# An attention and two-MLP kernel with an early expert pass: seven buffers for words to convert, evenly spaced conversions, earlier transposes, 240 rows

## The chip, the core and the metric

The kernel runs on one core of a Trainium2 chip. The core has five engines, each with its own queue that is worked off in order: PE (matrix multiply), DVE (vector), ACT (activations), POOL (GpSimd) and SP, which here only issues DMA transfers. The metric is the device time of one execution in microseconds (us), taken as the median of several runs.

## What is computed

The inputs are drawn once; two of the weights, `moe2_w_in` and `moe2_w_out`, come as float64. Cut to what matters:

```
scores = q @ k^T / 8; scores below (row maximum - tau) are masked; softmax; attn @ v      # 4 x 8 heads, 576 x 64
x = attention output as 2304 tokens x 512
logits = x @ w_gate; e = argmax(logits) over 8 experts; gate = softmax(logits)[e]
x[tokens of e] = gate * (relu(x[tokens of e] @ w1[e]) @ w2[e])                            # 512 -> 1024 -> 512
h = x @ w_in; out = (h - tanh(h)) @ w_out                                                 # 512 -> 2048 -> 512
```

Matrix products keep float32 accuracy by splitting each operand into a high and a low part and adding three products.

## The kernel before

**Attention** comes first, step by step (`Attn.run`), with the logits of the first and then the second half of the tokens behind it. A table of hooks (`Mlp.hooks`) puts work of the later stages between its last steps: the key (21, 0) is step 21 of the last head pair, place 0.

**The early pass.** When the first half of the tokens has its logits, the kernel picks the expert with the most tokens there (`pick` to `pick5`), gathers `NE` of its rows by an indirect DMA that POOL issues (`gather_exp`), transposes them on PE (`trans`), splits them into high and low parts on ACT and DVE (`evac`, into the tiles that `x_exp` makes) and sends them through that expert. This fills the time in which DVE works out the routing of all tokens (`route`, a generator whose pieces stand between the early pass's matmuls in `Mlp.run`).

**The expert stage.** `Mlp.run` then loops over steps `g`. Steps 8 to 71 are eight expert passes of eight steps, with 240, 464, 384, 352, 320, 288, 272 and 240 rows. In each step PE does 12 matmuls for a hidden tile `h`, ACT and DVE turn it into `hbuf` (relu, high and low part; lines 1301 and 1302), and PE does 12 matmuls for `y` of the tile two steps back. `h` has two banks in PSUM, `hbuf` three places; the transposed rows of the next pass go through one bank `t` (line 1238) that ACT and DVE empty (lines 1248, 1252).

**The last stage.** Steps 72 to 167 (GE is 72) are the second MLP, in six blocks of 16 steps: 12 matmuls for `h`, nine for `y`, and a polynomial for h - tanh(h) on ACT, DVE and POOL.

**What is put between the matmuls** is set by `plan`, which hangs functions on steps with `at(step, ...)`, by the numbers in the table `TB`:
- the weights: a load on SP (`wload`, line 1214, into one of four `raw` buffers), then two or three steps later the split (`wsplit`: cast on ACT, line 1222; low part on DVE or POOL, line 1226). The entry `last` does this for the 16 pieces of the last stage, which SP reads back from a scratch in memory (`wscr`, line 1200)
- 32 conversions of float64 words to float32 (`conv`), which fill `wscr`. Conversion n has four parts at set steps after its first: `load` (SP, line 1371: 512 KB into a `cv` buffer), `bits` (DVE, lines 1381, 1383, 1385), `sign` (ACT line 1389, DVE line 1390, POOL line 1392: the product goes to one half of the tile `cm`, even n one half, odd n the other) and `store` (SP, line 1395). Before, the parts stand 0, 3, 4 and 5 steps after the first, and there are three `cv` buffers.

Each engine's queue is in order, so one function that waits holds up all that stand behind it on its engine, those of later steps too.

Of the kernel before, what the change touches and what calls it, by code (L numbers as in the profile page):

```python
# [11 lines left out]
F32 = mybir.dt.float32  # L12
F32R = mybir.dt.float32r
# [3 lines left out]
U32 = mybir.dt.uint32  # L17
AF = mybir.ActivationFunctionType
ALU = mybir.AluOpType
# [4 lines left out]
B, H, S, D = 4, 8, 576, 64  # L24
# [410 lines left out]
E, F1, F2 = 8, 1024, 2048  # L435

CAPS = [240, 464, 384, 352, 320, 288, 272, 240]
NE = 256
NH = 9
NCH = [(c + 127) // 128 for c in CAPS]  # L440
CB = [sum(NCH[:r]) for r in range(E)]
# [4 lines left out]

PASS = [(-1, 0, NE)] + [(r, 0, n) for r, n in enumerate(CAPS)]
NTP = NT + max(CAPS)
# [26 lines left out]
class Moe:  # L475
# [110 lines left out]

    def hilo(self, T, x):
        V = self.nc.vector
        ab = T([128, 2, NTL], I32)
        V.tensor_scalar(out=ab[:, 0], in0=x, scalar1=7, scalar2=None, op0=ALU.logical_shift_right)  # L590
# [20 lines left out]

    def pick2(self, T):
        V, tt, red = self.nc.vector, self.tt, self.red
# [14 lines left out]
    def pick3(self):  # L628
# [15 lines left out]
        V.tensor_scalar(out=loi, in0=loc, scalar1=127, scalar2=None, op0=ALU.bitwise_and)  # L644
        V.scalar_tensor_tensor(out=vl, in0=loc, scalar=float(NE), in1=vl, op0=ALU.is_lt, op1=ALU.mult)
        V.tensor_copy(lo, loi)
# [16 lines left out]
    def pick5(self):  # L663
# [8 lines left out]
        red(self.ne, c)  # L672
        self.nc.vector.tensor_scalar(out=self.ne, in0=self.ne, scalar1=float(NE), scalar2=None, op0=ALU.min)

# [322 lines left out]
CORD = [(i + 8 * j, h) for i in (4, 5, 0, 1, 2, 3, 6, 7) for j in range(2) for h in range(2)]  # L997
# [28 lines left out]
class Mlp(Moe):  # L1026
    def hooks(self):
        T = lambda: Carve(self.sp.tile([128, 1024], F32R, tag="we", name="pick", bufs=4).bitcast(F32))
        sp = lambda i, j, eng: self.wsplit(-1, i, j, eng)
        return {(9, 0): [self.open1, lambda: self.best(0)],  # L1030
                (10, 2): [lambda: self.pick(self.psum)],
                (11, 0): [lambda: self.pick2(T()), self.wearly],
                (12, 0): [self.pick3],
                (14, 2): [lambda: self.pick4(self.psum), lambda: [self.gather_exp(0, m, 128) for m in range(2)]],
                (15, 0): [self.pick5],
                (17, 0): [lambda: self.wcast(-1, 0, 0), lambda: self.wlow(-1, 0, 0, self.nc.gpsimd)],
                (21, 0): [lambda: self.wcast(-1, 1, 0)],
                (21, 1): [lambda: self.wlow(-1, 1, 0, self.nc.vector)]}

    def open1(self):  # L1040
        self.cl.close()
# [22 lines left out]
    def run(self):  # L1064
        nc, tc = self.nc, self.tc
# [3 lines left out]
        self.ab = self.cp.tile([128, 2], F32, name="kna")  # L1069
        for i in range(2):  # L1070
            nc.gpsimd.memset(self.ab[:, i:i + 1], self.kn[2 * i])
        self.keep = sp.tile([128, 3072], F32, tag="lxa", name="keep")
        self.free = sp.tile([128, max(6 * NMAX, 8 * NW)], F32, tag="lxb", name="free")
        K = Carve(self.keep)
# [2 lines left out]
        hx = lambda f: self.hs.__setitem__(("p", f), self.h_exp(0, f))  # L1077
# [1 line left out]
        cast = lambda i, j: self.wcast(-1, i, j)  # L1079
        low = lambda i, j, eng: self.wlow(-1, i, j, eng)  # L1080
        next(r)
        for m in range(2):
            self.trans(("e", 0, m), 128)
        next(r)
        self.x_exp(0)
        for m in range(2):
            self.evac(("e", 0, m), 128 * m, 128)
        cast(2, 0)
        hx(0)
        hx(1)  # L1090
        next(r)
        rl(0)
# [43 lines left out]
        for m in range(2):  # L1136
            w = min(128, n1 - 128 * m)
# [5 lines left out]
        tg = iter([("we", 4)] * 4 + [("cv", 3)] * 3 + [("cm", 1)] + [("raw", 4)] * 4)  # L1143
# [119 lines left out]

    def x_exp(self, p):
        N = PASS[p][2]
        per = 1024 // N
        v = []
        for k0 in range(0, 4, per):
            nk = min(per, 4 - k0)
            v.append((k0, *(self.sp.tile([128, 1024], F32R, tag="xa", name="xa", bufs=8)[:, 0:nk * N]  # L1270
                            .rearrange("p (k w) -> p k w", k=nk) for _ in range(2))))
        self.xs["e", p] = v

# [87 lines left out]
            ap=self.tok2.bitcast(U32)[:, c:c + 1], axis=0))  # L1361


    def conv(self, i, h):
        nc = self.nc
        T = 3.4332275390625e-05
        st = {}

        def load():
            t = self.sp.tile([128, 1024], F32R, tag="cv", name="cv", bufs=3).bitcast(U32)  # L1370
            nc.sync.dma_start(out=t.rearrange("p (a b) -> p a b", a=2) if i < 8 else t, in_=self.src64[i][h])
            r = t.rearrange("p (n t) -> p n t", t=2)
            st["lo"], st["hi"] = r[:, :, 0], r[:, :, 1]
            st["hf"] = st["hi"].bitcast(F32)
            if self.cm is None:
                self.cm = self.sp.tile([128, 1024], F32R, tag="cm", name="cm")
            st["m"] = self.cm.bitcast(F32)[:, 512 * h:512 * h + 512]

        def bits():
            m = st["m"].bitcast(U32)  # L1380
            nc.vector.tensor_scalar(out=m, in0=st["hi"], scalar1=3, scalar2=0x40000000,  # L1381
                                    op0=ALU.logical_shift_left, op1=ALU.bitwise_xor)
            nc.vector.scalar_tensor_tensor(out=st["lo"], in0=st["lo"], scalar=29, in1=m,  # L1383
                                           op0=ALU.logical_shift_right, op1=ALU.bitwise_or)
            nc.vector.tensor_scalar(out=st["m"], in0=st["hf"], scalar1=-T, scalar2=None, op0=ALU.is_le)

        def sign():
            c = st["lo"].bitcast(F32)
            nc.scalar.activation(out=c, in_=c, func=AF.Abs)
            nc.vector.scalar_tensor_tensor(out=st["m"], in0=st["hf"], scalar=T, in1=st["m"],  # L1390
                                           op0=ALU.is_ge, op1=ALU.subtract)
            nc.gpsimd.tensor_tensor(out=st["m"], in0=st["lo"].bitcast(F32), in1=st["m"], op=ALU.mult)  # L1392

        def store():
            nc.sync.dma_start(out=self.wscr[i, :, 512 * h:512 * h + 512], in_=st["m"])

        return [load, bits, sign, store]


# [67 lines left out]
    def act2(self, g):  # L1467
# [4 lines left out]
        else:  # L1472
# [5 lines left out]


    TB = {"wl": (4, 5), "ws": (2, 3), "ga": 10, "tr": 7, "ev": 7,  # L1480
          "last": ((-3, -2), (-1, 1), (-2, 0), (0, 2), (-1, 2), (0, 3), (1, 2), (4, 6), (-56, -52), (-52, -49), (-7,
                  -1), (-6, -4), (5, 10), (9, 11), (11, 12), (12, 14)), "x0": (12, 9, 7), "x": (14, 13, 8),
          "conv": (0, 1, 3, 5, 7, 10, 11, 13, 15, 16, 18, 20, 21, 23, 25, 28, 29, 32, 33, 35, 37, 38, 40, 42, 44, 46,
                  47, 51, 52, 54, 57, 57), "cv": (0, 3, 4, 5), "eng": "DPDPDPDPDPPDDDPP"}

    def plan(self, K):
        at = self.at
        B = self.TB
        for p, (r, c0, n) in list(enumerate(PASS))[2:]:
            g = 8 * p  # L1490
            at(g - 8, self.x_exp, p)
            o = 2 if p == 2 else 0
            for m in range(-(-n // 128)):
                w = min(128, n - 128 * m)
# [5 lines left out]
        for r in range(E):  # L1500
            g = 8 * (r + 1)
# [9 lines left out]
        for k in range(NB):  # L1511
            g = GE + 16 * k
# [8 lines left out]
        for i, fn in enumerate(late):  # L1521
            at(14 + 2 * i, fn)
        for n, g in enumerate(B["conv"]):
            g = 8 + round(g * 49 / 57)
            for o, fn in zip(B["cv"], self.conv(*CORD[n])):
                at(g + o, fn)


# [44 lines left out]
```

## Time and profile before

| | |
|---|---|
| median of 3 runs | 1099.51 us (1099.19 to 1099.64) |
| the profiled execution | 1099.72 us, 0.21 above that median |
| its span, first to last instruction | 1097.7 us; 2.0 us lie around it |
| PE busy | 963.4 us (88%) |
| DVE busy | 907.2 us (83%) |
| POOL busy | 737.6 us (67%) |
| ACT busy | 678.1 us (62%) |
| granted TensorE clock, mean | 0.948 of full speed |

Busy shares are means over stages with different limits, and a matmul's busy time holds some of its waiting. So the profile is read by stage: which engine has no gaps there, and what ended the gaps of the others. The granted clock has two levels here, 0.5 and 1.0 of 2.4 GHz.

### The profile page before, as it was taken

The page shows a single profiled execution, that of the slowest core. Times are in us where ns is not written, and L with a number is a line of the kernel's source. Part 1 is how long each engine was busy: PE and PEld are TensorE (multiplying, and loading weights), DVE is VectorE, ACT ScalarE, POOL GpSimd, SP SyncE. Part 2 cuts the span into 40 slices and gives each one's busy share as a digit, 9 for nine tenths or more (in the row PEclk, how much of TensorE's full clock was granted, in tenths as well). Part 3 has the DMA queues.
Part 4 walks back from the last instruction along what each step waited for, and adds up shares of the span by engine and source line. Part 5 has one row for each costly group of instructions (what it writes and reads, how often), then busy time and mean ns, then how long its engine had stood idle before and what let it go on. Part 6 is the DMA issues. An engine that isn't in the chain of part 4 may idle for free. (4 is left out here: it accounts for less than half of the span.)

```text
span 1097.7 us, 20801 instructions
## 1 busy us (share of the span) xinstructions
PE 963.4 (88%) x7349; PEld 876.9 (80%) x7349; DVE 907.2 (83%) x1677; ACT 678.1 (62%) x1266; POOL 737.6 (67%) x646
## 2 busy tenths in 40 slices
PE   4687878868887979988979779999999999999997
PEld 4576767767776978888979778888999999999886
DVE  4899879979986859788868766998988989889894
ACT  5697987977973444344444447676656666656662
POOL 2897886877874345645555548887767768677673
PEclk9698998998987899999989999999999999999999
DMA  6698998998899479677778676420100101000000
GB/s 157 139 211 168 205 213 160 209 201 162 155 176 238 154 233 294 218 237 262 232 225 288 222 267 211 115 90 12 42 15 31 35 11 41 16 30 1 20 10 30
DMA packets 250569, 157.37 MB, mean 143 GB/s; under 512 B 179754, under 2 KB 224188, under 8 KB 250461
## 3 DMA queue, kind: packets, MB, share of 16 engines
q1 hardware_dynamic: 246701, 145.22, 52.6%
q0 software_dynamic: 3312, 10.49, 2.8%
q8 instruction: 59, 0.97, 0.4%
q10 hardware_dynamic: 448, 0.30, 0.1%
q14 instruction: 49, 0.40, 0.1%
HBM read 89.28 MB, written 23.60 MB: 103 GB/s over the span
## 5 line engine op out<-in xcount | busy, mean ns | idle before, releaser
L266 POOL TENSOR_TENSOR e<-em,e 128x1024 f16<-128x1024 f32 (+1 forms) x98 | 158.0, 1612 | 56.0 <-ACT e L262 31.0
L1459 POOL TENSOR_SCALAR tm<-u 128x384 uint8<-128x384 f32 x88 | 128.8, 1464 | 50.6 <-ACT u L1455 50.0
L1261 PE MATMUL h<-xa,w 128*128 128x240 f32 (+7 forms) x816 | 139.8, 323 | 22.6 <-DVE hbuf L1302 12.5
L1261 PEld LDWEIGHTS h<-xa,w 128*128 128x128 f32 x816 | 126.9, 201 | 28.9 <-DVE hbuf L1302 9.4
L241 ACT ACTIVATE e<-sps,n 128x576 f32<-128x576 f32 x144 | 110.9, 770 | 35.8 <-DVE n L235 30.7
L1321 PE MATMUL y<-hbuf,w 128*128 128x240 f32 (+6 forms) x768 | 129.5, 319 | 0.0
L1226 POOL TENSOR_TENSOR w<-raw,w 128x1024 fp32r<-128x1024 f32 x38 | 98.3, 2589 | 36.8 <-ACT w L1222 29.4
L1462 DVE SCALAR_TENSOR_TENSOR w<-y,w 128x384 f32<-128x384 f32 x96 | 123.0, 1281 | 0.0
L254 DVE SCALAR_TENSOR_TENSOR em<-sps,n,e 128x576 f32<-128x576 f32 x144 | 117.1, 813 | 6.8 <-ACT e L241 3.4
L1455 ACT ACTIVATE u<-h 128x384 f32<-128x384 f32 x96 | 47.1, 490 | 118.9 <-PE h L1261 118.9
L1321 PEld LDWEIGHTS y<-hbuf,w 128*128 128x128 f32 x768 | 117.4, 196 | 2.3
L235 DVE TENSOR_REDUCE n<-sps 128x1 f32<-128x576 f32 x144 | 107.3, 745 | 9.8 <-PE sps L227 9.6
L1261 PE MATMUL h<-xk,w 128*128 128x384 f32 x576 | 109.8, 338 | 2.9 <-DVE w L1226 2.7
L1476 POOL TENSOR_TENSOR gl<-w,gh 128x384 fp32r<-128x384 f32 x83 | 84.9, 1023 | 39.2 <-ACT gh L1475 39.2
L1261 PEld LDWEIGHTS h<-xk,w 128*128 128x128 f32 x576 | 102.1, 188 | 7.9 <-DVE w L1226 3.6
L298 PE MATMUL ops<-vh,et 128*128 128x64 f16 (+1 forms) x2240 | 96.2, 201 | 11.9 <-DVE x L304 11.0
L1392 POOL TENSOR_TENSOR cm<-cv,cm 128x512 f32<-128x512 f32 x32 | 46.4, 1454 | 87.5 <-issue 21.7
L298 PEld LDWEIGHTS <-et 128*128 128x128 f16 (+1 forms) x2240 | 82.8, 106 | 24.2 <-issue 19.8
L262 ACT CAST e<-em 128x576 f16<-128x576 f32 x144 | 100.4, 698 | 2.5 <-DVE em L254 1.2
L1222 ACT CAST w<-raw 128x1024 fp32r<-128x1024 f32 x80 | 83.8, 1052 | 21.6 <-DMA raw<-in_moe_w_dram 20.1
L227 PE MATMUL sps<-ka,qa 128*128 128x288 f32 x320 | 86.1, 362 | 9.1 <-DVE em L254 4.6
L1463 DVE SCALAR_TENSOR_TENSOR w<-y,w 128x384 f32<-128x384 f32 x96 | 77.6, 809 | 10.0
(267 smaller groups left out, 2336.2 us busy)
## 6 DMA issues: line engine op xcount, KB each, us to landing
raw<-in_moe_w_dram SPq DMA_DIRECT2D x72, 512.0 KB
cv<-in_moe_w_in_dram SPq DMA_DIRECT2D x16, 512.0 KB
cv<-in_moe_w_out_dram SPq DMA_DIRECT2D x16, 512.0 KB
wscr<-cm SPq DMA_DIRECT2D x32, 256.0 KB
raw<-wscr SPq DMA_DIRECT2D x16, 512.0 KB
xw<-yT SPq DMA_DIRECT2D x24, 192.0 KB
vv<-in_v_dram SPq DMA_DIRECT2D x8, 512.0 KB
raw<-in_q_dram SPq DMA_DIRECT2D x6, 576.0 KB
```

Source lines behind the costliest of these rows:

```text
L227: nc.tensor.matmul(ps[:, c, 0:288], lhsT=w[:, o:o + 128], rhs=ka[:, j, 288 * c:288 * c + 288], start=(i == 0), stop=(i == n - 1))
L235: nc.vector.tensor_reduce(out=n[:, 0:1], in_=ps[:, :, 0:288], axis=AX.XY, op=ALU.max, negate=True)
L241: nc.scalar.activation(out=e, in_=ps[:, :, 0:288], func=AF.Exp, bias=n[:, 0:1])
L254: nc.vector.scalar_tensor_tensor(out=self.em[u, g][:, i].rearrange("p (a b) -> p a b", a=2), in0=ps[:, :, 0:288], scalar=n[:, 1:2], in1=e, ...
L262: self.nc.scalar.copy(self.e16[u, g][:, i, 0:S], self.em[u, g][:, i])
L266: eng.tensor_tensor(out=e16[:, r, S + 64:], in0=em[:, r, 0:512], in1=e16[:, r, 0:512], op=ALU.subtract)
L298: nc.tensor.matmul(o[q], lhsT=et[:, base + c, q], rhs=vh[:, a, j, c if c < 5 else c - 5, :], start=(n == 0), stop=(n == len(terms) - 1))
L1226: eng.tensor_tensor(out=l, in0=raw, in1=h.bitcast(F32), op=ALU.subtract)
L1261: self.nc.tensor.matmul(out, lhsT=a, rhs=b, start=(i == 0), stop=(i == len(parts) - 1))
L1321: nc.tensor.matmul(self.ys[d], lhsT=a[:, f % 2, s], rhs=b, start=(f == 0 and i == 0), stop=(f == 7 and i == 2))
L1459: nc.gpsimd.tensor_scalar(out=mk, in0=u, scalar1=RCUT * RCUT, scalar2=None, op0=ALU.is_gt)
L1462: V.scalar_tensor_tensor(out=w, in0=y, scalar=b, in1=w, op0=ALU.add, op1=ALU.mult)
```

## The change

Five edits in one:
- **Buffers for conversions.** Conversion n loads into one of the three `cv` buffers when n % 7 is 0, 1 or 2, and otherwise into one of the four `we` buffers, which held weights of the early pass and, from early in the expert stage, two pieces of the last stage's weights. Those two pieces (entries 8 and 9 of `last`, 512 KB each) are now loaded nine and eight steps ahead of the last stage (steps 63 and 64) and split two steps later, in place of steps 16 and 20.
- **Spacing.** The first steps of the 32 conversions are 8 + n*14//9, and `bits`, `sign`, `store` come 4, 5 and 6 steps later.
- **The sign of every fourth conversion.** For n % 4 == 3, two `Sign` activations on ACT and an addition on POOL make the sign, and the comparisons of lines 1385 and 1390 on DVE are left out.
- **Rows transposed earlier.** The transposes of the early pass's rows stand in the hook (20, 1), their split in (21, 2), and the first hidden tile of the early pass ahead of the routing's first matmuls. The split rows lie in `yo` tiles.
- **240 rows.** `NE` falls from 256 to 240: the matmuls of the early pass have 240 columns. The other rows go with the later passes, whose sizes are fixed.

```diff
-NE = 256
+NE = 240
...
+                (20, 1): [lambda: self.x_exp(0), lambda: [self.trans(("e", 0, m), NE - 128 if m else 128) for m in range(2)]],
...
+                (21, 2): [lambda: [self.evac(("e", 0, m), 128 * m, NE - 128 if m else 128) for m in range(2)]]}
...
         next(r)
-        for m in range(2):
-            self.trans(("e", 0, m), 128)
+        hx(0)
         next(r)
-        self.x_exp(0)
-        for m in range(2):
-            self.evac(("e", 0, m), 128 * m, 128)
         cast(2, 0)
-        hx(0)
         hx(1)
...
-    def conv(self, i, h):
+    def conv(self, n, i, h):
...
+        sg = n % 4 == 3
...
-            t = self.sp.tile([128, 1024], F32R, tag="cv", name="cv", bufs=3).bitcast(U32)
+            tg, b = ("cv", 3) if n % 7 < 3 else ("we", 4)
+            t = self.sp.tile([128, 1024], F32R, tag=tg, name="cv", bufs=b).bitcast(U32)
...
-            nc.vector.tensor_scalar(out=st["m"], in0=st["hf"], scalar1=-T, scalar2=None, op0=ALU.is_le)
+            if not sg:
+                nc.vector.tensor_scalar(out=st["m"], in0=st["hf"], scalar1=-T, scalar2=None, op0=ALU.is_le)
...
-            nc.scalar.activation(out=c, in_=c, func=AF.Abs)
-            nc.vector.scalar_tensor_tensor(out=st["m"], in0=st["hf"], scalar=T, in1=st["m"],
-                                           op0=ALU.is_ge, op1=ALU.subtract)
+            if sg:
+                nc.scalar.activation(out=st["m"], in_=st["hf"], func=AF.Sign, bias=self.tt2[:, 0:1])
+                nc.scalar.activation(out=st["hf"], in_=st["hf"], func=AF.Sign, bias=self.tt2[:, 1:2])
+            nc.scalar.activation(out=c, in_=c, func=AF.Abs, scale=0.5 if sg else 1.0)
+            if sg:
+                nc.gpsimd.tensor_tensor(out=st["m"], in0=st["m"], in1=st["hf"], op=ALU.add)
+            else:
+                nc.vector.scalar_tensor_tensor(out=st["m"], in0=st["hf"], scalar=T, in1=st["m"],
+                                               op0=ALU.is_ge, op1=ALU.subtract)
...
-          "last": ((-3, -2), (-1, 1), (-2, 0), (0, 2), (-1, 2), (0, 3), (1, 2), (4, 6), (-56, -52), (-52, -49), (-7,
+          "last": ((-3, -2), (-1, 1), (-2, 0), (0, 2), (-1, 2), (0, 3), (1, 2), (4, 6), (-9, -7), (-8, -6), (-7,
...
-                  47, 51, 52, 54, 57, 57), "cv": (0, 3, 4, 5), "eng": "DPDPDPDPDPPDDDPP"}
+                  47, 51, 52, 54, 57, 57), "cv": (0, 4, 5, 6), "eng": "DPDPDPDPDPPDDDPP"}
...
-            g = 8 + round(g * 49 / 57)
-            for o, fn in zip(B["cv"], self.conv(*CORD[n])):
+            g = 8 + n * 14 // 9
+            for o, fn in zip(B["cv"], self.conv(n, *CORD[n])):
```

How the order on the engines moves is shown at three places. Lines of the changed kernel stand one to eleven higher (1381, 1383, 1385, 1390 are now 1385, 1387, 1390, 1401; 1252 is 1253, 1302 is 1304).

DVE in the pass of 320 rows, before. The rows named `xa` empty the bank `t` of transposed rows, `cm` and `cv` belong to conversions:

```order
L1390 SCALAR_TENSOR_TENSOR cm<-cv,cm 128x512 x2
L1302 SCALAR_TENSOR_TENSOR hbuf<-h,hbuf 128x320
L1252 TENSOR_TENSOR xa<-t,xa 128x3x128
L1252 TENSOR_TENSOR xa<-t,xa 128x128
L1381 TENSOR_SCALAR cm<-cv 128x512
L1383 SCALAR_TENSOR_TENSOR cv<-cv,cm 128x512
L1385 TENSOR_SCALAR cm<-cv 128x512
L1302 SCALAR_TENSOR_TENSOR hbuf<-h,hbuf 128x320
```

The same place of the change:

```order
L1304 SCALAR_TENSOR_TENSOR hbuf<-h,hbuf 128x320
L1253 TENSOR_TENSOR xa<-t,xa 128x3x128
L1253 TENSOR_TENSOR xa<-t,xa 128x128
L1401 SCALAR_TENSOR_TENSOR cm<-cv,cm 128x512
L1385 TENSOR_SCALAR cm<-cv 128x512
L1387 SCALAR_TENSOR_TENSOR cv<-cv,cm 128x512
L1304 SCALAR_TENSOR_TENSOR hbuf<-h,hbuf 128x320
```

Two signs that stood together are now one to a step, and this conversion, one of every fourth, has no third row in `bits`.

SP where the expert stage ends, before (`raw<-in_moe_w_dram` is a piece of expert weights, `raw<-wscr` one of the last stage, `wscr<-cm` a conversion's store):

```order
L1395 DMA wscr<-cm 128x512 x2
L1214 ISA
L1214 DMA raw<-in_moe_w_dram 128x2x512
L1214 ISA
L1214 DMA raw<-in_moe_w_dram 128x4x256
L1214 ISA
L1214 DMA raw<-in_moe_w_dram 128x2x512
L1200 DMA raw<-wscr 128x1024
```

The same place of the change:

```order
L1406 DMA wscr<-cm 128x512
L1215 ISA
L1215 DMA raw<-in_moe_w_dram 128x2x512
L1201 DMA raw<-wscr 128x1024
L1215 ISA
L1215 DMA raw<-in_moe_w_dram 128x4x256
L1201 DMA raw<-wscr 128x1024
L1215 ISA
L1215 DMA raw<-in_moe_w_dram 128x2x512
L1201 DMA raw<-wscr 128x1024
```

Two more reads of `wscr` stand between the last expert's weights.

PE where attention ends and the early pass begins, before (`lps` and `ops` belong to the logits, `y<-ident,xr` are the transposes, lines 693 and 694 the routing):

```order
L557 MATMUL lps<-ident,x 128x128 x3
L565 MATMUL ops<-wg,xT 128x8 x6
L1238 MATMUL y_6003<-ident,xr 128x128 x4
L1238 MATMUL y_6008<-ident,xr 128x128 x4
L693 LDWEIGHTS onesh
L693 MATMUL t<-O,onesh 128x152
```

The same place of the change:

```order
L1239 MATMUL y_5965<-ident,xr 128x128 x4
L1239 MATMUL y_5970<-ident,xr 128x112 x4
L565 MATMUL ops<-wg,xT 128x8 x3
L557 MATMUL lps<-ident,x 128x128 x3
L565 MATMUL ops<-wg,xT 128x8 x6
```

The transposes, which wait for the gathered rows, now stand ahead of the last nine logits matmuls, and 12 matmuls of the first hidden tile stand between these and line 693.

## Rows read from the trace of the kernel before

**Rows 1.** Windows by stage: busy us (instructions) PE, PEld, DVE, ACT, POOL; clock; DMA.

```profile
387.00:651.00 264.00, 226.46 (x1440) 216.37 (x1440) 207.37 (x296) 117.84 (x210) 140.80 (x80) 0.95 0.76 250
651.00:690.00 39.00, 36.26 (x276) 34.65 (x275) 24.51 (x32) 26.41 (x48) 29.39 (x17) 1.00 0.68 219
690.00:1098.00 408.00, 395.51 (x1961) 353.88 (x1960) 355.39 (x492) 246.64 (x510) 290.00 (x230) 0.99 0.10 31
```

**Rows 2.** What PE waited for, 387 to 690: us, times, longest.

```profile
PE t L1238 <- issue: 13.9, 4, 5.8
PE h L1261 <- DVE hbuf L1302: 12.5, 6, 3.1
```

**Rows 3.** Timeline at the longest of these gaps: start, us, what [idle before].

```profile
550.42 0.38 SPq L1371 DMA_DIRECT2D cv<-in_moe_w_in_dram  x1
...
558.15 0.43 DVE L1381 TENSOR_SCALAR cm<-cv 128x512 uint32<-128x512 uint32 x1 [7.87 <-issue]
...
560.94 0.60 PE L1238 MATMUL t<-ident,xr 32*128 32x32 f32 x4 [5.83 <-issue]
```

**Rows 4.** What DVE waited for at line 1381, 387 to 651.

```profile
DVE cm L1381 <- DMA wscr<-cm: 9.8, 3, 5.0
...
DVE cm L1381 <- issue: 8.5, 3, 7.9
DVE cm L1381 <- DMA cv<-in_moe_w_in_dram: 4.4, 1, 4.4
DVE cm L1381 <- POOL cm L1392: 2.2, 1, 2.2
```

**Rows 5.** What SP's queue waited for, 387 to 651.

```profile
SPq L1371 <- POOL cm L1392: 69.6, 12, 9.9
SPq L1395 <- POOL cm L1392: 60.0, 17, 8.6
```

**Rows 6.** Timeline of PE: four more gaps behind a late line 1381.

```profile
467.01 2.38 PE L1261 MATMUL h<-xa,w 128*128 128x384 f32 x12 [2.76 <-DVE hbuf L1302]
...
489.31 3.91 PE L1261 MATMUL h<-xa,w 128*128 128x384 f32 x12 [2.06 <-DVE hbuf L1302]
...
580.33 0.50 PE L1261 MATMUL h<-xa,w 128*128 128x288 f32 x2 [1.31 <-DVE hbuf L1302]
...
607.09 0.50 PE L1261 MATMUL h<-xa,w 128*128 128x288 f32 x2 [3.09 <-DVE hbuf L1302]
```

**Rows 7.** Windows at clock 0.5: sums of four after 489, then two (414, 646).

```profile
sum 17.09, PE 13.81 PEld 13.78 DVE 14.73 ACT 5.49 POOL 9.25; mean PE 3.45 PEld 3.45 DVE 3.68 ACT 1.37 POOL 2.31
...
sum 6.83, PE 6.52 PEld 6.52 DVE 6.14 ACT 2.86 POOL 5.32; mean PE 3.26 PEld 3.26 DVE 3.07 ACT 1.43 POOL 2.66
```

**Rows 8.** Groups of instructions, 387 to 651: parts of the conversions.

```profile
L1385 DVE TENSOR_SCALAR cm<-cv 128x512 f32<-128x512 f32 x32 | 31.8, 994 | 1.1
L1390 DVE SCALAR_TENSOR_TENSOR cm<-cv,cm 128x512 f32<-128x512 f32 x32 | 29.1, 920 | 0.0
...
L1389 ACT ACTIVATE cv<-cv 128x512 f32<-128x512 f32 x32 | 21.8, 681 | 40.3 <-issue 27.8 <-POOL cm L1392 5.1 <-DVE cv L1383 4.8
...
L1392 POOL TENSOR_TENSOR cm<-cv,cm 128x512 f32<-128x512 f32 x32 | 46.4, 1454 | 87.5 <-issue 21.7 <-ACT xa L1248 16.2 <-DVE cm L1390 16.2
```

**Rows 9.** Timeline of DVE and POOL at 642.

```profile
642.29 2.50 DVE L1385 TENSOR_SCALAR cm<-cv 128x512 f32<-128x512 f32 x1
...
645.89 0.43 DVE L1385 TENSOR_SCALAR cm<-cv 128x512 f32<-128x512 f32 x1
...
642.01 2.50 POOL L1226 TENSOR_TENSOR w<-raw,w 128x1024 fp32r<-128x1024 f32 x1 [4.97 <-ACT w L1222]
```

**Rows 10.** Timeline where the early pass begins: PE, and DVE's first slack.

```profile
353.56 1.64 PE L565 MATMUL ops<-wg,xT 128*128 128x8 f32 x12
...
355.98 0.88 PE L1238 MATMUL y<-ident,xr 128*128 128x128 f32 x4 [0.29 <-DMA xr<-rows,idx]
...
361.70 0.43 DVE L1302 SCALAR_TENSOR_TENSOR hb<-h,hb 128x256 fp32r<-128x256 f32 x1 [1.50 <-ACT hb L1301]
```

**Rows 11.** Chain that ended last: a read of `wscr` near the stages' border.

```profile
667.17 4.35 DMA raw<-wscr
```

More of the change, by code (lines that the diff above doesn't have):

```diff
@@ L1033, in hooks @@
                 (12, 0): [self.pick3],
-                (14, 2): [lambda: self.pick4(self.psum), lambda: [self.gather_exp(0, m, 128) for m in range(2)]],
+                (14, 2): [lambda: self.pick4(self.psum), lambda: [self.gather_exp(0, m, NE - 128 if m else 128) for m in range(2)]],
                 (15, 0): [self.pick5],
                 (17, 0): [lambda: self.wcast(-1, 0, 0), lambda: self.wlow(-1, 0, 0, self.nc.gpsimd)],
+                (20, 1): [lambda: self.x_exp(0), lambda: [self.trans(("e", 0, m), NE - 128 if m else 128) for m in range(2)]],
                 (21, 0): [lambda: self.wcast(-1, 1, 0)],
-                (21, 1): [lambda: self.wlow(-1, 1, 0, self.nc.vector)]}
+                (21, 1): [lambda: self.wlow(-1, 1, 0, self.nc.vector)],
+                (21, 2): [lambda: [self.evac(("e", 0, m), 128 * m, NE - 128 if m else 128) for m in range(2)]]}
     def open1(self):
@@ L1071, in run @@
             nc.gpsimd.memset(self.ab[:, i:i + 1], self.kn[2 * i])
+        T = float(np.nextafter(np.float32(3.4332275390625e-05), np.float32(0)))
+        self.tt2 = self.cp.tile([128, 2], F32, name="knt")
+        for i in range(2):
+            nc.gpsimd.memset(self.tt2[:, i:i + 1], T if i else -T)
         self.keep = sp.tile([128, 3072], F32, tag="lxa", name="keep")
@@ L1265, in x_exp @@
         N = PASS[p][2]
-        per = 1024 // N
+        w, tg, b = (1024, "xa", 8) if p else (512, "yo", 4)
+        per = w // N
         v = []
@@ L1269, in x_exp @@
             nk = min(per, 4 - k0)
-            v.append((k0, *(self.sp.tile([128, 1024], F32R, tag="xa", name="xa", bufs=8)[:, 0:nk * N]
+            v.append((k0, *(self.sp.tile([128, w], F32R, tag=tg, name="xa", bufs=b)[:, 0:nk * N]
                             .rearrange("p (k w) -> p k w", k=nk) for _ in range(2))))
```

## The prediction

> **What bounds the kernel now.** I read the windows by stage first, since the page's 88% for PE is a mean. From 690 us to the end PE is busy for 395.5 of 408 us: that stage is PE's own, and nothing in the diff makes its matmuls fewer. In the expert stage, 387 to 651 us, PE is busy for 226.5 of 264 us, DVE for 207.4, and no engine is full [rows 1]. Time can be had there, 37.5 us of idle PE at the most, and what PE loses at the lower clock.
>
> The list of what PE waited for says where it went. Four transposes into the bank `t` waited 13.9 us and six hidden tiles 12.5 us for `hbuf` from DVE [rows 2]. The transposes' releaser is shown as "issue", but the largest can be followed by hand: SP issues a conversion's load at 550.42, DVE sits idle for 7.87 us until it can start that conversion's `bits` at 558.15, then empties the bank `t`, and PE, idle for 5.83 us, transposes at 560.94 [rows 3]. DVE is in order, so a conversion that is late holds back `xa` and `hbuf`, which PE needs now, though nobody needs the conversion itself before the last stage. The load was late because its buffer was in use: SP stood 69.6 us, 12 times, at line 1371 until POOL had finished a product from the same three buffers, and 60.0 us at the stores [rows 5]. DVE's idle time at line 1381 has two more causes: three times, 9.8 us, the store out of the same half of `cm` had not landed, and once, 2.2 us, POOL's product was late; the late words are the 8.5 and 4.4 us beside them [rows 4].
>
> So I sort PE's 26.4 us (13.9 + 12.5) into two shares. **Share A**, gaps behind an idle line 1381: 2.76 + 2.06 + 1.31 + 3.09 [rows 6] and 5.83 [rows 3], 15.05 us. **Share B**, the other 11.35 us, five gaps in which DVE was not idle but had several conversion parts in a row. Behind six of the gaps the granted clock was 0.5, the level of 1.2 GHz, and PE worked at it for 13.81 us after gaps of A and 6.52 us after gaps of B [rows 7]; at the full clock that is half, so 6.9 and 3.3 us go with them. A is 22.0 us, B 14.6.
>
> **The change, part by part.** *Seven buffers.* Loads n and n-7 of one buffer lie 10 or 11 steps apart, and its product is taken 5 steps after the load: the wait at line 1371 goes. The store's wait stays, one step behind the product as before, and what is queued behind it on SP is the next weights, as now. *Spacing.* Conversions n and n-2 share a half of `cm`. Before, their first steps lie 2 apart in six cases, so that `bits` comes one step after the product that has yet to be stored; after, always 3 or 4, and `bits` comes at least two steps after it. Those are the conditions behind all of A. Its bounds are 0 (the next late thing takes the place: weights, or the same stores) and 22.0. I take four fifths, 17.6: each of the five gaps loses its cause, but DVE still works at 79% here (207.4 of 264), and I let one of five come back at another place.
>
> *The sign of every fourth.* Eight conversions lose lines 1385 and 1390 on DVE, 8 x (0.994 + 0.920) = 15.3 us [rows 8]; ACT gains 16 activations like line 1389, 16 x 0.681 = 10.9 us, and POOL 8 additions like line 1392, 8 x 1.454 = 11.6 us [rows 8]. ACT (117.8 of 264) and POOL (140.8) have room [rows 1]. Behind the longer ACT part stand the next `hbuf` and the next cast, behind POOL's the next gather or low part; this cover is one step, and if it is gone each of the eight puts its 2 x 0.681 + 1.454 = 2.8 us on PE. Spacing and lighter DVE together work on B, whose bounds are 0 and 14.6. I take a third, 4.9: the two parts' 60.9 us (31.8 + 29.1 [rows 8]) fall by a quarter, and the rest of B's crowding is `xa`, low parts and routing, which stay.
>
> How far DVE is relieved depends on POOL. Of two equal instructions at line 1385, the one that begins at 642.29 lasts 2.50 us beside a POOL low part that begins at 642.01 and lasts 2.50, and the one at 645.89, with POOL idle, 0.43 us [rows 9]. The Trainium skill, Advanced Engine Details and Errata, section VectorE Performance Modes, says that DVE's second SBUF port is shared with GpSimd and that the two block each other; the trace agrees with its 2.50 against 0.43 us. By that rule work moved from DVE to POOL comes partly back as blocked time: the eight additions could take up to 11.6 of the 15.3 us. The sum by the row alone is that of the forecast; by the rule it is the second rival.
>
> *The two pieces moved to the end.* Steps 63 and 64 now each load two pieces, and steps 65 and 66 as before. In 651 to 690 us DMA is at 0.68 and PE at 36.3 of 39 us [rows 1], and a read of `wscr` there stood 4.35 us on the chain that ended last [rows 11]. Bounds: 0, if the queue has room, and 2 x (4.35 + 2.50) = 13.7 us, if both come in line with a landing [rows 11] and a low part of POOL's length [rows 9]. One MB at 219 GB/s would be 4.8 us of transfer, and the engines have idle time for part of it; I take 3.5 lost. What the early steps gain by losing them I take as nothing: 1 MB of the 66 MB that 264 us at 250 GB/s carry.
>
> *Early pass.* The last logits ended at 353.56 + 1.64 = 355.2. Now they stand behind transposes of which the second waits for its rows until 355.98 and takes 0.88 [rows 10]; the twelve matmuls of 1.64 us then end by about 358.5, 3.3 us later, and with them the routing on DVE. Against that DVE had 1.50 us of slack at 361.70 [rows 10], and 192 matmuls lose 16 columns each, at 2.4 GHz 192 x 16 / 2400 = 1.3 us. Bounds -1.3 and +3.3; I take 3.3 - 1.5 - 1.3 = +0.5. The extra constants and 16 rows that go with later passes of fixed size cost nothing: no pass grows.
>
> **Sum.** -17.6 - 4.9 + 3.5 + 0.5 = -18.5 us against the profiled execution's 1099.72 (span 1097.7 and 2.0 around it), so 1081.2; that execution lies 0.2 above the median of the runs, so the forecast is **1081.0 us**. Its own range, one gap of A more or less and B from 0 to two thirds, is 1074 to 1088.
>
> **Rivals.** All times are on the scale of the median.
> - *DVE and POOL stay in each other's way.* The additions take back what DVE was spared, and B stays whole: -17.6 + 4.0 = -13.6, 1085.9 us. For it speaks the 2.50 us instruction [rows 9]; against it that at most eight parts are involved, and spacing works without them.
> - *The end pays.* Both moved pieces come in line, 13.7 us, and PE's stop brings one stretch of 3.4 us at the lower clock, 1.7 more: -17.6 - 4.9 + 0.5 + 13.7 + 1.7 = -6.6, 1092.9 us. For it: the chain already runs over such reads [rows 11]. Against: DMA is idle for a third there.
> - *Both shares go whole:* -22.0 - 14.6 + 4.0 = -32.6, 1066.9 us. For it: every gap of both has conversions in it. Against: weights' landings lie close behind.
> - *The wait only moves.* The halves of `cm` are still two, and if their stores (9.8 us of DVE's 24.9 us idle at line 1381 [rows 4]) take up what the words leave, A stays and only B's third and the costs are left: -4.9 + 4.0 = -0.9, 1098.6 us. Against: two steps, some 9 us (264 us are 56 steps), for a product and a store.
> - *Slower: the Sign conversions stall PE.* At each of the eight places ACT holds the next `hbuf` back, and PE waits 2.8 us: 22.6 us, so -18.5 + 22.6 = +4.1, 1103.6 us; with a stretch at the lower clock behind each, 1.7 more, 1117. It decides from 18.5 / 8 = 2.3 us a place. Against: ACT is busy for 45% of the stage, and PE's two banks of `h` give it a step.
>
> **Chances.** Forecast 0.46, blocked DVE 0.16, the end 0.14, both whole 0.10, the wait moves 0.06, slower 0.08. A range from 1066 to 1094 us holds the first four but for their edges and leaves the last two out; beyond these bounds the cases have no more than about 0.2. A difference of 0.2% (2.2 us) is about what a measurement of this kernel can tell from no change. Faster by more: 0.46 + 0.16 + 0.14 + 0.10 = 0.86; within it 0.06; slower 0.08.
>
> **What would show it.** Right: SP's wait at line 1375 (was 1371) near nothing; DVE's idle time at line 1385 (was 1381) under 5 us from 24.9; the transposes' 13.9 and `hbuf`'s 12.5 us together under 12; fewer stretches at clock 0.5; the last stage's steady part as long as now and beginning some 18 us earlier. Wrong: PE waits for casts or low parts of weights in place of `hbuf`; line 1385 idle until stores land; gaps between 630 and 690 that grow by more than 4 us; `hbuf` on ACT late behind pairs of Sign.

## The result, and the profile after

The changed kernel takes **1086.68 us** (median of 4 runs, 1084.18 to 1089.43) against 1099.58 us (4 runs) for the kernel before: a ratio of 0.9882, 95% interval 0.9855 to 0.9909, 12.9 us faster. The forecast was 1081.0, with a range from 1066 to 1094. The execution profiled is the fastest of the four, 1084.18 us with a span of 1081.9.

The window of the expert stage in the changed kernel, as in [rows 1] (columns: window, its length, busy us and instructions of PE, PEld, DVE, ACT, POOL; clock; DMA share; GB/s):

```profile
387.00:651.00 264.00, 239.63 (x1591) 227.77 (x1590) 230.90 (x292) 138.93 (x249) 167.30 (x95) 0.98 0.81 265
```

In the same 264 us PE is busy for 239.6 us where it was 226.5, at 0.98 of the full clock where it was 0.95. But DVE too is busy for longer, 230.9 us after 207.4, although the change took work off it.

Windows at fixed times mix steps once a kernel has shifted: the changed kernel is further on at 651 us, and part of DVE's longer work belongs to later steps. So I cut the profiled executions at the same matmuls: the end of attention's last product (line 298), the early pass's last matmul (it reads the hidden tile `hb`), the last expert's first hidden matmul (240 columns), the first output matmul of the last stage, and PE's last matmul. The cuts of the changed kernel, in the timeline of PE (start, us, what, and in brackets the idle time before it):

```profile
347.79 1.38 PE L298 MATMUL ops<-vh,et 128*128 128x64 f16 x42 [0.45 <-DVE x L304]
...
389.43 0.49 PE L1323 MATMUL h<-hb,w 128*128 128x240 f32 x3
...
630.43 0.39 PE L1262 MATMUL h<-xa,w 128*128 128x240 f32 x2
...
669.02 0.49 PE L1351 MATMUL y<-w,gh 128*128 128x512 f32 x1
...
1075.02 0.40 PE L1351 MATMUL y<-cv,gw 128*128 128x512 f32 x1
```

From the same cuts of all profiled executions, lengths in us ("border" is the stretch from the last expert's first matmul to the last stage's first output; what PE's last matmul leaves is 6.5 to 6.7 everywhere):

```
                              attention  early  expert  border   last
before                           352.06  34.19  264.97   33.12  406.69
after                            349.17  40.75  240.51   38.58  406.40
e1_transposes_back               350.75  34.05  242.26   39.23  406.44
e2_three_buffers                 350.85  39.07  250.06   37.31  406.39
e3_old_spacing                   352.54  38.83  252.59   43.39  406.51
e4_no_sign                       351.67  40.77  242.05   36.64  406.44
e5_before_even_spacing           350.47  36.05  253.55   32.81  406.71
e6_pieces_later                  351.95  38.26  241.17   34.66  408.82
e7_both                          352.36  33.89  242.02   34.97  408.85
e8_both_no_sign                  353.62  33.95  243.97   33.70  408.86
e9_product_on_dve                353.02  33.77  235.41   32.98  409.05
e10_all_sign                     353.82  34.73  250.33   34.93  408.72
e11_low_part_on_dve              351.21  37.84  241.45   38.88  406.41
e12_three_buffers_product_on_dve 349.06  34.19  245.97   33.04  406.74
```

So the change won 24.5 us in the expert stage and paid 6.6 in the early pass and 5.5 at the border: -24.5 + 6.6 + 5.5 - 0.3 = -12.7, where the medians differ by 12.9. The 2.9 us in attention are not counted as the change's: the six kernels with 240 rows and the transposes behind the logits (the first, seventh to tenth and twelfth run) have the same instructions up to there, and their attention ends between 349.1 and 353.8 us. Each length is that of one execution. Kernels that share a stage's code show how far one can vary: the expert stage of the changed kernel and of the first, sixth, seventh and eleventh run lies between 240.5 and 242.3 us, the last stage with the pieces early or at the border between 406.4 and 406.7, and the early pass in the changed order between 37.8 and 40.8. So a difference of 2 us in the expert stage, or of 3 us in the early pass of the changed order, can be chance.

**The expert stage.** Cut at the same matmuls, before and after (columns as above):

```profile
386.25:651.22 264.97, 226.94 (x1442) 216.88 (x1443) 207.59 (x296) 118.47 (x212) 141.65 (x81) 0.95 0.76 249
389.92:630.43 240.51, 220.19 (x1442) 209.10 (x1442) 213.50 (x277) 125.77 (x225) 150.11 (x87) 0.99 0.83 270
```

PE's idle time, the length less the busy time, falls from 38.0 to 20.3 us, and its mean clock rises from 0.95 to 0.99. DVE works for 5.9 us more on 19 instructions fewer. What DVE waited for at line 1385 (was 1381 [rows 4]) and SP at its longest, 387 to 651 us (columns: us in all, times, longest):

```profile
DVE cm L1385 <- POOL cm L1399: 0.9, 1, 0.9
DVE cm L1385 <- DMA wscr<-cm: 0.5, 1, 0.5
```

```profile
SPq L1406 <- POOL cm L1403: 122.9, 31, 6.6
SPq L1330 <- ACT yo L1326: 18.5, 10, 11.1
```

The 24.9 us of idle time ahead of `bits` are 1.4 us. The load (line 1375, was 1371 [rows 5]) has no row any more; SP's wait has moved to the store, 122.9 us where it was 60.0, with the next weights behind it; for a cast of weights PE waited once, 1.7 us. What PE waited for, 387 to 690 us, beside [rows 2]:

```profile
PE h L1262 <- DVE w L1227: 11.9, 10, 2.4
PE h L1262 <- DVE hbuf L1304: 5.3, 8, 1.4
PE t L1239 <- issue: 2.9, 2, 1.5
PE t L1239 <- DMA xr<-rows,idx: 1.8, 2, 1.1
PE h L1262 <- ACT w L1223: 1.7, 1, 1.7
```

Transposes and `hbuf` fell from 26.4 to 8.2 us. Low parts of weights from DVE rose from 6.1 to 11.9 us: DVE is late again, with something else. That is one of the signs of being wrong which the prediction named. Why DVE is busier, its conversion parts tell, beside [rows 8]:

```profile
L1387 DVE SCALAR_TENSOR_TENSOR cv<-cv,cm 128x512 uint32<-128x512 uint32 x32 | 51.5, 1608 | 1.1
...
L1401 DVE SCALAR_TENSOR_TENSOR cm<-cv,cm 128x512 f32<-128x512 f32 x24 | 31.0, 1292 | 0.0
```

Line 1401 (was 1390) runs 24 times in place of 32 and takes 31.0 us where it took 29.1; one lasts 1292 ns after 920. All four parts together take 132.0 us after 123.7.

**The early pass.** PE's timeline behind attention, beside [rows 10]:

```profile
352.83 0.66 PE L1239 MATMUL y<-ident,xr 128*128 128x128 f32 x4 [3.29 <-DMA xr<-rows,idx]
354.68 1.01 PE L1239 MATMUL y<-ident,xr 112*128 112x112 f32 x4 [1.19 <-DMA xr<-rows,idx]
355.48 1.31 PE L565 MATMUL ops<-wg,xT 128*128 128x8 f32 x6
356.64 0.88 PE L557 MATMUL lps<-ident,x 128*128 128x128 f32 x3
357.31 2.57 PE L565 MATMUL ops<-wg,xT 128*128 128x8 f32 x12
```

and the clock behind it, from the windows:

```profile
355.50:362.40 6.90, 6.90 (x34) 6.85 (x33) 2.17 (x8) 2.02 (x4) 0.00 (x0) 0.50 0.66 185
```

PE stands 4.5 us before rows that are still in flight, and then takes 2.57 us for the twelve logits matmuls that took 1.64, at a granted clock of 0.50, which is 1.2 GHz. The kernel before has a stretch at 0.50 here too, but behind its logits; the changed one has more of it. The whole early pass, cut as above, before, after, and in the first run below:

```profile
352.06:386.25 34.19, 33.07 (x252) 30.74 (x251) 27.36 (x73) 16.69 (x27) 11.13 (x10) 0.90 0.54 177
349.17:389.92 40.75, 34.84 (x253) 33.26 (x251) 27.41 (x75) 16.68 (x29) 12.13 (x13) 0.83 0.44 139
350.75:384.80 34.05, 31.87 (x253) 29.76 (x251) 27.33 (x75) 16.58 (x29) 10.75 (x11) 0.90 0.55 179
```

PE's idle time grows from 1.1 to 5.9 us. A mean clock of 0.90 over 34.19 us is 6.8 us at 0.5, and 0.83 over 40.75 us is 13.9; the 7.1 us more cost half of that, 3.5. With 1.3 us less for narrower matmuls this would be 4.8 + 3.5 - 1.3 = 7.0; the pass is 6.6 us longer.

**The border.** DVE, POOL and PE where PE waits longest:

```profile
642.99 2.37 POOL L1227 TENSOR_TENSOR we<-raw,we 128x1024 fp32r<-128x1024 f32 x1 [0.57 <-ACT we L1223]
643.09 3.36 DVE L1227 TENSOR_TENSOR w<-raw,w 128x1024 fp32r<-128x1024 f32 x1
...
646.50 1.77 PE L1262 MATMUL h<-xa,w 128*128 128x240 f32 x10 [2.40 <-DVE w L1227]
```

`we` is a piece that the change moved here. Its low part on POOL lies beside one of the last expert's on DVE, which takes 3.36 us where the next one, at 651.74, takes 1.23, and PE waits for that. Over the whole border PE is idle for 4.9 us where it was 1.5.

### The profile page after: what moved, and what is told of

The parts are those of the page before. It is cut to its first block, busy times and chain, and to the rows that moved or that the text cites. A ratio compares the mean times of both kernels' runs of the same rounds, so it can differ in the third digit from the quotient of the medians.

```text
span 1081.9 us, 20819 instructions
## 1 busy us (share of the span) xinstructions
PE 960.4 (89%) x7349; PEld 871.8 (81%) x7349; DVE 922.6 (85%) x1663; ACT 689.3 (64%) x1284; POOL 751.2 (69%) x656
## 5 line engine op out<-in xcount | busy, mean ns | idle before, releaser
L1262 PE MATMUL h<-xa,w 128*128 128x240 f32 (+6 forms) x816 | 135.7, 315 | 17.1 <-DVE w L1227 9.7
L1262 PEld LDWEIGHTS h<-xa,w 128*128 128x128 f32 x816 | 122.4, 194 | 23.4 <-DVE w L1227 11.6
L235 DVE TENSOR_REDUCE n<-sps 128x1 f32<-128x576 f32 x144 | 107.2, 744 | 11.1 <-PE sps L227 11.1
L1351 PE MATMUL y<-w,gh 128*128 128x512 f32 x258 | 81.6, 397 | 1.7 <-POOL w L1227 1.3
```

Source lines behind the costliest of these rows:

```text
L235: nc.vector.tensor_reduce(out=n[:, 0:1], in_=ps[:, :, 0:288], axis=AX.XY, op=ALU.max, negate=True)
L1262: self.nc.tensor.matmul(out, lhsT=a, rhs=b, start=(i == 0), stop=(i == len(parts) - 1))
L1351: nc.tensor.matmul(self.ys[m], lhsT=a[:, s], rhs=b[:, f % 2], start=(f == 0 and i == 0), stop=(f == 15 and i == 2))
```

## The experiments

All times are medians; each ratio is to the runs of the kernel before on the same chip, with its 95% interval. Multiplied by 1099.6 a ratio gives a time that can be set beside 1086.7.

**Transposes back.** The calls of `x_exp`, `trans`, `evac` and the first `hx` as in the kernel before, 240 rows kept (lines behind it count 3 higher):

```diff
-                (20, 1): [lambda: self.x_exp(0), lambda: [self.trans(...) ...]],
-                (21, 2): [lambda: [self.evac(...) ...]]}
...
         next(r)
-        hx(0)
+        for m in range(2):
+            self.trans(("e", 0, m), NE - 128 if m else 128)
         next(r)
+        self.x_exp(0)
+        for m in range(2):
+            self.evac(("e", 0, m), 128 * m, NE - 128 if m else 128)
         cast(2, 0)
+        hx(0)
```

> The changed kernel with the early pass's transposes, copies and first hidden tile back behind the last logits (still 240 rows). Theory: in the changed kernel PE waits 3.29 and 1.19 us for the gathered rows ahead of the last logits and then works through 21 logits matmuls at the lower clock, and the early pass ends 3.7 us later than before although attention ended about 2.3 us earlier in that execution, so 6.0 us are lost there. Put back, the loss goes, and the 1.3 us of the 240 rows come on top: 1086.7 - 7.3 = about 1079.4 us. Rival: the rows' landing is on the path in either order, and PE waits for them behind the logits instead: 1085 to 1087 us.

1082.45 us, ratio 0.9833 (0.9810 to 0.9856): 5.4 us faster than the changed kernel. The early pass is 34.05 us long again; no other stage differs by more than 1.8 us from the changed kernel. In its timeline

```profile
352.25 1.64 PE L565 MATMUL ops<-wg,xT 128*128 128x8 f32 x12
353.96 0.66 PE L1242 MATMUL y<-ident,xr 128*128 128x128 f32 x4
355.73 1.01 PE L1242 MATMUL y<-ident,xr 112*128 112x112 f32 x4 [1.11 <-DMA xr<-rows,idx]
```

the logits cover all but 1.11 us of the rows' flight and run at the full rate. The theory holds, but for the credit of the 240 rows: the early pass with them is 0.1 to 0.4 us shorter than before in four runs (this one and the seventh to ninth), as long in the twelfth and 0.5 longer in the tenth, not 1.3 shorter. The windows above say where it went: PE's busy time does fall from 33.07 to 31.87 us, at the same mean clock, but it is idle for 1.1 us more.

**Three buffers.**

```diff
-            tg, b = ("cv", 3) if n % 7 < 3 else ("we", 4)
+            tg, b = "cv", 3
...
-"cv": (0, 4, 5, 6)
+"cv": (0, 3, 4, 5)
```

> The changed kernel with three buffers for words (and the old 3, 4 and 5 steps from load to bits, product and store); even spacing, Sign and the rest stay. Theory 'the spacing does it': load n+3 comes 4 or 5 steps after load n, whose product is taken after 4, so three buffers just suffice; SP's wait at the load is short and the time stays at 1086 to 1089 us. Rival 'the buffers do it': loads wait for products again, words come late, and about half of the 22.0 us of share A comes back: 1095 us or more.

1094.16 us, 0.9935 (0.9908 to 0.9963), 5.8 us slower than the changed kernel. The expert stage is 250.1 us, so 9.6 of the 24.5 us need the buffers with the longer steps that they allow (the two were taken back together), and both sides expected too clean a split. The store's wait is back on DVE, and the load's on SP:

```profile
DVE cm L1385 <- DMA wscr<-cm: 13.7, 8, 3.4
```

```profile
SPq L1375 <- POOL cm L1403: 64.7, 10, 8.4
```

**The old spacing.**

```diff
-            g = 8 + n * 14 // 9
+            g = 8 + round(g * 49 / 57)
```

> The changed kernel with the old, uneven table of conversion steps; seven buffers, Sign and the rest stay. Theory 'the spacing does it': six conversions come two steps behind the one whose half of cm they need, DVE waits for stores (9.8 us in the kernel before) and the parts bunch up: 1092 to 1097 us. Rival 'the buffers do it': words are on time, stores are covered: 1086 to 1088 us.

1101.10 us, 1.0007 (0.9989 to 1.0025): the whole gain is gone. The expert stage still gives 12.4 of its 24.5 us, so the change without its spacing, seven buffers among it, does help there; DVE waits 11.1 us for stores. The other loss is at the border, 43.4 us long, where the old table's last conversions (five first steps from 52 to 57) meet the two moved pieces. Which of the two holds the other up was not taken apart.

**No Sign.**

```diff
-        sg = n % 4 == 3
+        sg = False
```

> The changed kernel with all 32 conversions in the old form (no Sign on ACT, no additions on POOL). Theory: the Sign form gave nothing, since DVE's conversion parts take 132.0 us in the changed kernel (51.5 + 31.0 + 25.4 + 24.1) against 123.7 before, although 16 of them are gone; without it 1085 to 1089 us. Rival: it does relieve DVE where it is crowded, and its loss costs PE 15.3 us of DVE work in part, about a third: 1091 to 1093 us.

1086.09 us, 0.9875 (0.9853 to 0.9897): no difference from the changed kernel. 1.5 us more in the expert stage, 1.9 less at the border. The four conversion parts take 140.3 us on DVE here (51.9 + 37.2 + 27.7 + 23.5) and 132.0 with the Sign form, so it does spare DVE 8.3 of the 15.3 us, and PE gains nothing by it.

**The kernel before with even spacing.** The kernel before, one line:

```diff
-            g = 8 + round(g * 49 / 57)
+            g = 8 + n * 14 // 9
```

> The kernel before with one line changed: conversions evenly spaced, 14 steps for nine. Three buffers, no Sign, 256 rows, old transposes, the two pieces of the last stage loaded early as before. Theory 'spacing and buffers each give their part': the expert stage gives what it gave in the run with three buffers (250.1 against 265.0 us, -14.9), nothing is paid in the early pass or at the border of the stages: 1099.6 - 14.9 = about 1085 us, so one line is worth as much as the whole change. Rival: the conversions need the two later pieces' buffers or the Sign form, or the weights' queue, and less than half comes: 1092 us or more.

1088.45 us, 0.9883 (0.9850 to 0.9916): one line is worth as much as the five edits together. The expert stage gives 11.4 us, less than with three buffers above, and nothing is paid at the border. Line 1371 still waits (63.1 us), and so does `bits` for the stores:

```profile
DVE cm L1381 <- DMA wscr<-cm: 11.1, 6, 3.7
```

**The two pieces later.**

```diff
-          "last": (..., (4, 6), (-9, -7), (-8, -6), (-7,
+          "last": (..., (4, 6), (3, 5), (5, 8), (-7,
```

> The changed kernel with the two moved pieces of the last stage loaded 3 and 5 steps after that stage begins (cast after 5 and 8), in place of 9 and 8 steps ahead of it. Theory: the 5.5 us lost between the last expert's first matmul and the last stage's first output matmul come from these two pieces, whose low parts meet the last expert's on DVE and POOL; away from there the loss goes, the last stage (DVE busy for 0.87 of it) takes them in: 1086.7 - 5.5 = about 1081 us. Rival: the last stage has no room either, and PE waits there instead: 1086 us or more; with the pieces late at steps 8 and 10 even 1090.

1084.48 us, 0.9849 (0.9815 to 0.9884). The border is 3.9 us shorter, but the last stage 2.4 us longer, so the price is mostly moved and little of 5.5 us is left; against the changed kernel the intervals overlap. In the last stage PE waits for POOL behind the pieces, 1.0 us more than in the changed kernel (1.4, 4 times); the rest of the 2.4 us stays open:

```profile
PE y L1351 <- POOL gl L1487: 2.4, 5, 0.9
```

**Both,** transposes back and pieces later:

> The changed kernel with the transposes back behind the last logits and the two pieces later, the two edits that each undo a loss. Theory: they add, -5.4 (measured) and -5.5: about 1076 us. Rival: what is saved ahead of the last stage is given back in it: 1081 to 1082 us, as with the transposes alone.

1079.66 us, 0.9806 (0.9775 to 0.9838), 8.4 us faster than the changed kernel. The border gives 4.3 us against the run with the transposes alone, the last stage takes 2.4 back: between the two expectations.

**Both, without Sign:**

> The same without the Sign form (all 32 conversions as before). Theory: the Sign form is worth nothing, within 2 us of the run with it: 1074 to 1078 us. Rival: with the pieces gone from the border DVE is what PE waits for in the expert stage (low parts of weights, 12 us), and the Sign form's relief shows: 3 us or more slower without it.

1080.17 us, 0.9804 (0.9772 to 0.9837): the Sign form is worth nothing here either.

**The product on DVE,** in the kernel of the last run (this part stands in line 1406 there):

```diff
-            nc.gpsimd.tensor_tensor(out=st["m"], in0=st["lo"].bitcast(F32), in1=st["m"], op=ALU.mult)
+            nc.vector.tensor_tensor(out=st["m"], in0=st["lo"].bitcast(F32), in1=st["m"], op=ALU.mult)
```

> The kernel of the last run (transposes back, pieces later, no Sign) with the conversions' 32 products on DVE in place of POOL. Theory 'DVE and POOL block each other': in the changed kernel a word part at line 1387 takes 0.69 us when POOL computes nothing beside it (7 of 32) and 1.86 us on average when it does (25 of 32); taking 43.5 us of products off POOL frees about as much of DVE's blocked time as the 32 products add (32 x 0.7 = 22 us), and the mean of the word parts falls from 1.49 to 1.1 us or less: 1076 to 1082 us, the same within noise or a little faster. Rival 'DVE is the bound by its own work': 22 us more on an engine that is busy for 88% of the stage go to PE in good part, 1090 us or more.

1072.67 us, 0.9739 (0.9715 to 0.9763): the fastest kernel of this study, 15.7 us below the changed one by the ratios and better than even this theory said. The conversion's parts on DVE in the run before it, without the products,

```profile
L1390 DVE SCALAR_TENSOR_TENSOR cv<-cv,cm 128x512 uint32<-128x512 uint32 x32 | 47.7, 1492 | 1.1
...
L1404 DVE SCALAR_TENSOR_TENSOR cm<-cv,cm 128x512 f32<-128x512 f32 x32 | 41.0, 1280 | 0.0
...
L1393 DVE TENSOR_SCALAR cm<-cv 128x512 f32<-128x512 f32 x32 | 27.6, 864 | 1.1
L1388 DVE TENSOR_SCALAR cm<-cv 128x512 uint32<-128x512 uint32 x32 | 23.1, 722 | 1.1 <-POOL cm L1406 1.1
```

and with them:

```profile
L1406 DVE TENSOR_TENSOR cm<-cv,cm 128x512 f32<-128x512 f32 x32 | 36.2, 1131 | 3.9 <-ACT cv L1400 1.0
L1404 DVE SCALAR_TENSOR_TENSOR cm<-cv,cm 128x512 f32<-128x512 f32 x32 | 31.7, 992 | 0.0
...
L1390 DVE SCALAR_TENSOR_TENSOR cv<-cv,cm 128x512 uint32<-128x512 uint32 x32 | 28.6, 894 | 1.2
L1393 DVE TENSOR_SCALAR cm<-cv 128x512 f32<-128x512 f32 x32 | 24.4, 761 | 1.1
L1388 DVE TENSOR_SCALAR cm<-cv 128x512 uint32<-128x512 uint32 x32 | 19.1, 598 | 0.0
```

Four parts took 139.4 us; five parts, 32 instructions more, take 140.0. The second number behind the bar tells why: each of the old four got shorter, the word part from 1492 to 894 ns. POOL's busy time fell to 110.4 us of 264. Nothing but the engine of that product was changed, so it is shown that POOL's work lengthens DVE's. The low parts on DVE, 128x1024 each, fell as well, from 1525 to 1288 ns. In the cut of the expert stage PE's idle time falls from 22.3 to 15.4 us with it.

**All with Sign,** the seventh run's kernel with `sg = True`:

> The kernel with transposes back and pieces later, and with all 32 conversions in the Sign form in place of 8. Theory 'blocked': another 48 parts leave DVE, but POOL's 24 more additions (24 x 1.37 = 33 us) block the parts that stay, whose mean rises; DVE's conversion time falls by 22 us at most, and the time stays at 1077 to 1083 us, or rises by POOL's and ACT's own load. Rival 'DVE's work counts': the 12 us for which PE waits on low parts and hbuf halve, 1073 us or less.

1087.61 us, 0.9873 (0.9849 to 0.9897), 7.4 us slower than with eight. The rival falls: DVE's conversion time did fall, from 132.1 to 95.3 us (57.5 + 37.8), and PE gained nothing. The theory 'blocked' is not right either: it allowed 22 us at most, DVE was spared 36.8, and the time rose. The word part got longer still,

```profile
L1390 DVE SCALAR_TENSOR_TENSOR cv<-cv,cm 128x512 uint32<-128x512 uint32 x32 | 57.5, 1798 | 1.1
```

and ACT, in order too, stood before the Sign for words that DVE had not done, with the next `hbuf` behind it:

```profile
ACT cm L1398 <- DVE cv L1390: 34.1, 21, 4.4
```

With eight of them that row has 7.2 us, 4 times. DVE's wait for `hbuf` from ACT rose from 27.3 to 45.6 us. So far this is the prediction's "slower" rival, at four times the dose. But PE's own wait for `hbuf` did not grow (5.4 us, and 5.6 with eight); it waits longer at the transposes, 5.9 and 4.9 us where the run with eight has 1.9 and 2.9:

```profile
PE t L1242 <- DMA xr<-rows,idx: 5.9, 3, 3.1
PE t L1242 <- issue: 4.9, 3, 2.0
```

Which engine's delay brings that about was not taken apart; POOL, which issues the gathers of those rows, is busy for 195.3 of 264 us after 166.6.

**A low part on DVE.**

```diff
-"eng": "DPDPDPDPDPPDDDPP"
+"eng": "DPDPDPDPDDPDDDPP"
```

> The changed kernel with the low part of the second moved piece on DVE in place of POOL (one letter of the table). Theory: at the border one low part of the last expert took 3.36 us on DVE beside that piece's low part on POOL, PE stood 2.40 us behind it and then worked at the lower clock; with both on DVE, one behind the other, each takes about 1.2 us and the border gets 1 to 3 us shorter (from 38.6 us). Rival: the order of the pieces costs it, not the block; the extra 1.2 us on DVE leave it at 38.6 us or make it longer.

1086.83 us, 0.9872 (0.9846 to 0.9897); the border is 38.9 us, not shorter. The theory named the right pair and the wrong remedy:

```profile
643.16 1.21 DVE L1227 TENSOR_TENSOR w<-raw,w 128x1024 fp32r<-128x1024 f32 x1
...
645.60 2.93 POOL L1227 TENSOR_TENSOR w<-raw,w 128x1024 fp32r<-128x1024 f32 x1 [0.37 <-ACT w L1223]
...
646.24 2.71 DVE L1428 TENSOR_TENSOR xw<-xw,xr 128x384 f32<-128x384 f32 x1
...
649.32 0.98 PE L1262 MATMUL h<-xa,w 128*128 128x240 f32 x5 [2.16 <-DVE hbuf L1304]
```

The low part takes 1.21 us now, but DVE is then later, its next scaling of rows meets POOL's next low part, and PE waits 2.16 us behind that.

**Three buffers again, product on DVE,** the two pieces early as in the kernel before:

> Of the change only the even spacing and the 240 rows are kept: three buffers (and the old 3, 4 and 5 steps), no Sign, transposes behind the logits, the two pieces of the last stage loaded early as in the kernel before; and the product of the conversions is on DVE. Theory 'seven buffers are still needed': words come late again when load n+3 waits for a product; 8 to 10 us of the 29.6 us of the run with the product on DVE are lost, while the 2.4 us that the later pieces cost in the last stage come back: 1072.7 + 9 - 2.4 = about 1079 us. Rival 'POOL was what held the words back': with the product on DVE three buffers do, and the time is 1068 to 1073 us.

1079.83 us, 0.9823 (0.9801 to 0.9844), as the theory had it. Against the ninth run the expert stage loses 10.6 us and the last stage gets 2.3 back. SP's wait at the load is there with DVE as releaser, so the buffers, with their steps, are needed whoever makes the product:

```profile
SPq L1378 <- DVE cm L1388: 63.0, 10, 8.4
```

## Why the prediction came out as it did

It was right in sign and range, 5.7 us too low, and in its sum two errors cancel and a third remains.

- **Late words and even spacing (A and B, -22.5).** Measured -24.5. The step held: `bits` waits 1.4 us, the load not at all, transposes and `hbuf` 8.2 us, under the 12 that were named. That buffers and spacing both stand behind it is shown by leaving one out: about -12 us with either alone (-12.4 with the buffers, -11.4 and -14.9 with the spacing). But alone only spacing paid: the buffers with the old table, and the pieces at the border, lost there what they won.
- **"Spacing and lighter DVE together work on B."** The half with lighter DVE failed. DVE did not get lighter: the conversion's four parts take 132.0 us in the changed kernel (51.5 + 31.0 + 25.4 + 24.1) against 123.7 in the kernel before, 16 instructions fewer. The Sign form itself spares DVE 8.3 us (140.3 without it); the other edits lengthen the same parts by 16.6, and the run with the products on DVE shows that POOL's work beside them can do that. Leaving the Sign form out changes nothing, twice. The rival "DVE and POOL stay in each other's way" had the mechanism, but only some half of the 15.3 us came back, and its 1085.9 us is close to the measured time; but that is chance, since it put -17.6 on the expert stage and +4.0 on the costs, and these were -24.5 and +11.8.
- **The two pieces at the end (+3.5).** Measured +5.5, within the bounds. What was mis-sized is the meeting of low parts on DVE and POOL, which I had as an upper bound only. Most of the price is there wherever the pieces go: 3.9 to 4.3 us come back at the border and 2.4 go in the last stage.
- **The early pass (+0.5, bounds -1.3 and +3.3).** This step failed: +6.6 in the profiled execution, 3.7 to 6.6 in the six with this order (the fifth run, in the old order, has 1.9 more than the kernel before with PE idle for only 0.6 us, at a mean clock of 0.83, so some of that is spread). I let the second transposes wait until 355.98 as before and the logits then run in 1.64 us. But what covered the rows' flight in the kernel before was the logits; moved behind it, they leave PE idle for 4.5 us, and some 7 us more of the pass run at the lower clock, the logits among them with 2.57 us for 1.64. The 1.3 us for narrower matmuls came as 1.2 us of busy time, and with the old order 1.1 us more of idle time took them.

By term: -22.5 became -24.5, +3.5 became +5.5, +0.5 became +6.6; the first two errors cancel, and the third, +6.1, is about the difference to the forecast.

## What to carry to other kernels

When a long stall ends with a wait for a buffer, look at how the work that fills it is spaced before adding buffers: here one line of even spacing was worth as much as the five edits. A move that pulls work ahead of a wait must say what covered that wait until now. And work that moves from DVE to POOL is to be charged to DVE as well: take a DVE instruction's duration with POOL idle and with POOL busy from the trace, and try the move in the other direction too, which gave the fastest kernel here.

## What the runs showed of the hardware

- A word part on DVE (two inputs from SBUF, 128x512) takes 0.69 us or waits for POOL, by what POOL does when it begins. In the changed kernel 18 of 32 begin while a POOL computation runs; they take 1.66 to 2.79 us and end 0.55 us behind POOL's instruction (one is shown below). Of the 14 others, 13 take 0.69 us, also where POOL begins during them or only issues a gather; one takes 4.45. `hbuf` parts, of which one input comes from PSUM, take 0.40 to 0.64 us in the 16 cases that begin beside a POOL computation and 0.39 to 0.64 in the 48 others. The counts of 7 and 25 in the ninth run's expectation take a POOL instruction within 0.4 us of the word part as beside it. The Trainium skill, Advanced Engine Details and Errata, section VectorE Performance Modes, speaks of two-port VectorE instructions and GpSimd instructions that block each other; the runs agree for VectorE's side, and show it for instructions with two tensors from SBUF as well.

```profile
452.02 2.59 POOL L1227 TENSOR_TENSOR w<-raw,w 128x1024 fp32r<-128x1024 f32 x1
452.38 2.77 DVE L1387 SCALAR_TENSOR_TENSOR cv<-cv,cm 128x512 uint32<-128x512 uint32 x1
```

- Putting 32 products from POOL on DVE left the sum of DVE's conversion parts as it was, 139.4 and 140.0 us.
- With the same instructions up to there, attention's last product ended between 349.1 and 353.8 us in six executions. A difference of 5 us between two single profiles of this kernel says nothing before it is cut by stage.
